# FFN middle tiles copied out of PSUM first, late loads issued after the first U transpose, and one shared tile for the last FFN slice of two chunks

## The chip, the cores and the metric

The kernel runs on one core of a Trainium2 chip. The metric is the device time of one execution in microseconds (us). The kernel before takes 736.66 us as the median of 10 runs (735.02 to 740.17). Five engines work side by side, each through its own list of instructions in order: TensorE (PE in the profile, with its weight loads as PEld), VectorE (DVE), ScalarE (ACT), GpSimd (POOL) and SyncE (SP, which here issues nearly all DMAs). [...]

## The reference

One layer with attention and a feed-forward network (FFN) in parallel on the same normalised input. S = 2048 tokens, D = 640, H = 32 query heads of width 20 that share one key head and one value head, F = 1728.

```
xn  = layernorm(x)                                  # over D, no weights
q   = xn @ wq  -> 32 heads x 20;  k = xn @ wk;  v = xn @ wv
o   = softmax(q k^T / sqrt(20)) v                   # per head, over all 2048 keys
out = x + o @ wo + silu(xn @ w1) @ w2               # w1 640x1728, w2 1728x640
```

The kernel writes silu(h) as 0.5 * h * (1 + tanh(h/2)); the factor 0.5 is applied later, with the residual.

## The kernel before

**Attention, the backbone.** The 2048 queries are cut into 4 chunks of 512 (QW). A unit is one head of one chunk, so there are 128 units, taken three at a time in 43 groups. A group walks over 16 key tiles of 128 (KT), which gives 688 steps. One step (`do_S`) issues three S matmuls (line 773), one per unit, into three PSUM banks, alternating between banks 0 to 2 and 3 to 5. The exponentials of the step are shared out. In a "narrow" step ACT takes two units in one 128x1024 activation (line 791), and DVE takes the third with an integer trick: one `tensor_scalar` out of PSUM (p1, line 805), an offset add on POOL (yp, line 811) and another on DVE for up to three steps at a time (y, `flush_z`, line 873). In a "wide" step ACT takes all three units in one 128x1536 activation and DVE takes none. `want_dve` decides: it adds up how far the planned DVE queue runs behind PE and takes the narrow form if that is below DVE_TH. Then the P·V matmuls (line 861) sum into the U bank (bank 6). At the end of a group DVE copies U to SBUF (`Uev`, line 976), SP issues a DMA transpose of it (`norm_dma`, line 935), POOL gathers the pieces (lines 943 to 948), DVE takes a reciprocal (line 953), and POOL scales (line 962).

**FFN and projections, the filling.** Between the attention steps PE runs jobs (class `Job`), each a chain of matmuls into bank 7, then a `consume` that takes the bank away. Per chunk there are 14 `h_job`s: 5 matmuls of w1 against xnT (line 1090) give a 128x512 tile of h, of which the last, fk = 13, has only 64 rows (FLAST). ACT takes its tanh out of PSUM into the buffer `tb` (line 1098, two slots) and DVE multiplies (line 1103, reading `tb` and PSUM) into `hT`. Bank 7 stays taken until both are done. Then 8 `out_job`s per chunk multiply hT with w2 (line 1152, read out at 1169), and 8 more, a chunk later, multiply the attention output with wo (line 1157, read out at 1187). `qd_job` (lines 1054 and 1061) makes the queries of the coming chunk.

**What sets the order.** `Sched` is a planner that runs when the kernel is built. Every operation has an assumed duration and a priority (a smaller number goes first), and each engine takes the ready operation with the smallest priority. The result is a fixed list per engine. On the chip a late operation holds up all that stands behind it on its engine. PE prefers P·V over jobs when more than NBLK - PV_PRESS of the 31 exponential blocks are in use. On SP, loads named "dma" keep their own order, while the small transposes may overtake them if they are ready and older.

**Late loads.** The FFN's w2 (14 DMAs), wo (5 DMAs) and a 1 MB pre-fill of the second query buffer (`qz(1)`, line 1512) can't start at once, because their SBUF space holds other data in the prologue. `late_loads` is called when the first `qd_job` (c = 0, m = 0) is read out, and waits for that read-out. Five POOL multiplications (line 1522) then scale wo by 2.

```
if c == 0 and m == 0:
    self.late_loads(("qd", sl))
```

Of the kernel before, what the change touches and what calls it, by code (L numbers as in the profile page):

```python
# [14 lines left out]
P = 128  # L15
# [30 lines left out]
NBLK = 31  # L46
NZ = 4
ZB = 3
AHEAD = 30
Q_FROM = 8  # L50
H0_STEP = 10
KT_ACT = ()
Y_POOL = True
Y_TIME = 0.72
Y_LOCK = False
# [5 lines left out]
ZWAIT = 6  # L61
SWITCH = 0.105
S_LEAD = 0.56
PV_PRESS = 8
DVE_TH = 2.6
U_PRIO = 1.1
X_PRIO = 0.8
PACE = (0.9, 0.9, 0.9, 0.9)
# [273 lines left out]


class Job:
    def __init__(self, name, mms, reads, consume, gate=None, min_step=-1, banks=None, on_start=None, width=0, hold=None, use=None):
        self.name = name
        self.mms = mms
        self.reads = reads
        self.consume = consume
        self.gate = gate  # L350
        self.min_step = min_step
        self.on_start = on_start
        self.begun = False
        self.width = width
        self.hold = hold
        self.use = use


class Builder:
# [371 lines left out]
    def do_mm(self, job, now, d):  # L731
        work, fn = job.mms.pop(0)
        job.begun = True
        b = job.bank
        op = self.sc.new("pe", d, lambda pe: fn(pe, b), job.reads, [("B", b)], name=job.name, queue=False)
        op.work = min(work, 0.009) if job.name[0] == "v" else min(work, 0.053) if job.name[0] == "t" else work
        self.pe_mode = "M"
        self.sc.commit(op, now)
        if not job.mms:
            self.cur_job = None  # L740
            job.consume(b)
# [12 lines left out]
    def do_S(self, t, now):  # L754
# [93 lines left out]
        if self.zblocks and (len(self.zblocks) >= (ZB if g < self.NG - 2 else 2) or t - self.zblocks[0][0] >= ZWAIT  # L848
                             or t == self.T - 1 or (kt == KT - 1 and g >= FLUSH_G)):
            self.flush_z()  # L850
        self.move_pv()
        if last:
            self.end_group(g)
# [10 lines left out]
    def flush_z(self):  # L864
# [12 lines left out]
        for i, (t, pv) in enumerate(self.zblocks):  # L877
# [10 lines left out]
                self.pv_mm(pe, 0, 3, kt, x, False, False)  # L888
                return self.pv_mm(pe, 1, 4, kt, x, False, False)
            ts.append((th, ("Y", zs, 1, i), kt))  # L890
        first = self.zblocks[0][1]
        end = self.pv_wait[-1][0].kt == KT - 1
        tail = self.pv_wait.pop() if end else None
        seen = False
# [21 lines left out]
            self.pv_wait.append((op, False))  # L916
        if tail is not None:
            self.pv_wait.append(tail)
        self.zblocks = []

    def can_host(self, op):
        return op.after is not None and not op.after and op.kt < KT
# [8 lines left out]
    def norm_dma(self, g, rows):  # L931
# [5 lines left out]
        op.dur = UT_ISSUE  # L937
        self.ut_cnt[up] += 1
        op.inc_no = self.ut_cnt[up]
        ut = self.UT[:, up, :, :].rearrange("p q (i j) -> p q i j", j=SLOT)  # L940
        w = self.W
        if rows == P:
# [104 lines left out]
    def qd_job(self, c, m, step=-1):  # L1047
        sc = self.sc
        lo, hi = (Q0 if c == 0 else QN)[m]
        rows = hi - lo  # L1050
        mms = []
        for k in range(DC):
            def f(pe, b, k=k):
                return pe.matmul(self.bk(b, 0, QW, 0, rows), self.wq[:, k, lo:hi], self.xnT[:, k, c * QW:(c + 1) * QW],  # L1054
                                 start=(k == 0), stop=(k == DC - 1))
            mms.append((t_mm(QW), f))

        def consume(b):
            sl = self.nqd % 2
            self.nqd += 1  # L1060
            sc.new("dve", t_dve_ps(QW), lambda v: v.tensor_scalar(self.qd[0:rows, sl, :], self.bk(b, 0, QW, 0, rows), C1,
                                                                  None, ALU.mult), [("B", b)], [("qd", sl)],
                   prio=X_PRIO, name=f"qev{c}_{m}")
            sem = sc.sem(f"q{c}_{m}")
            ops = []
            heads = range(lo // DH, -(-hi // DH))
            for h in heads:
                a, z = max(lo, h * DH), min(hi, h * DH + DH)
                r = (h % 4) * SLOT + a - h * DH
                ops.append(sc.dma("sp", lambda q, a=a, z=z, r=r, h=h: q.dma_start(  # L1070
                    self.qT[r:r + z - a, h // 4, c % 2, :], self.qd[a - lo:z - lo, sl, :]), [("qd", sl)],
                    [("qb", c % 2, h)], (z - a) * QW * 2, sem=sem, name="qdma"))
                ops[-1].dur = 0.74
            sc.note(ops[-1], (), [("q", c, h, lo) for h in heads])
            for op in ops:
                op.inc_no = len(ops)
            if c == 0 and m == 0:
                self.late_loads(("qd", sl))
        reads = [("xnT", 4 * c + i) for i in range(4)] + [("wqd", 0), ("wqd", 1)]
        if c >= 2:  # L1080
            step = max(step, self.first_step[c - 1] + KT)
        return Job(f"q{c}_{m}", mms, reads, consume, min_step=step, width=QW if rows == P else 0)

    def h_job(self, c, fk, step):
        sc = self.sc
        rows = P if fk < FC - 1 else FLAST
        mms = []
        for k in range(DC):
            def f(pe, b, k=k):
                return pe.matmul(self.bk(b, 0, QW, 0, rows), self.w1[:, k, fk * P:fk * P + rows],  # L1090
                                 self.xnT[:, k, c * QW:(c + 1) * QW], start=(k == 0), stop=(k == DC - 1))
            mms.append((t_mm(QW), f))

        def consume(b):
            tp = fk % 2
            t = self.tb[0:rows, tp, :]
            src = self.bk(b, 0, QW, 0, rows)
            sc.new("act", t_act(QW), lambda a: a.activation(t, src, AF.Tanh, scale=0.5), [("B", b)], [("tb", tp)],  # L1098
                   prio=X_PRIO, name=f"th{c}_{fk}")
            ks = [("hT", fk)]  # L1100
            if c == 0:
                ks += [("hT_x", i) for i in range(self.XS)]
            sc.new("dve", t_dve_ps(QW), lambda v: v.scalar_tensor_tensor(  # L1103
                out=self.hT[0:rows, fk, :], in0=t, scalar=1.0, in1=src, op0=ALU.add, op1=ALU.mult),
                [("B", b), ("tb", tp)], ks, prio=X_PRIO, name=f"hp{c}_{fk}")
        reads = [("xnT", 4 * c + i) for i in range(4)] + [("w1",)]
        return Job(f"h{c}_{fk}", mms, reads, consume, min_step=step, width=QW if rows == P else 0)

    def try_oT(self, c):
        last = c == QC - 1  # L1110
# [29 lines left out]
    def out_job(self, c, i, e, step=-1, ffn=True, ks=range(DC), src="xres", dst="ost", hmax=H):  # L1140
# [5 lines left out]
        tot = (FC if ffn else 0) + len(ks)  # L1146
        if ffn:
            for fk in range(FC):
                rows = P if fk < FC - 1 else FLAST

                def f(pe, b, fk=fk, rows=rows, m=len(mms)):
                    return pe.matmul(self.bk(b, 0, 320), self.hT[0:rows, fk, i * P:(i + 1) * P],  # L1152
                                     self.w2[0:rows, fk, e0:e0 + 320], start=(m == 0), stop=(m == tot - 1))
                mms.append((t_mm(320), f))
        for k in ks:
            def f(pe, b, k=k, m=len(mms)):
# [76 lines left out]
    def fill_chunk(self, c, t):  # L1233
# [8 lines left out]
        else:  # L1242
            for i in range(4):
                self.load_xres(0, i)
        hs = [(3.0, lambda s, fk=fk: self.h_job(c, fk, s)) for fk in range(FC)]
        if c == 0:
            qs.pop(0)
        ys = []
# [43 lines left out]
    def prologue(self):  # L1292
# [40 lines left out]
        w2p = []  # L1333
        for fk in range(FC):
            rows = P if fk < FC - 1 else FLAST
            w2p.append(lambda q, fk=fk, rows=rows: q.dma_start(self.w2[0:rows, fk, :],
                                                               self.B_w2[fk * P:fk * P + rows, :]))

        def load_w2(extra):
            load_w("sp", "2", w2p, ("w2",), P * D * 2, [("xn", i) for i in range(14)] + [("idf",)], extra)  # L1340
# [322 lines left out]
```

## Time and profile before

| | |
|---|---|
| median of 10 runs | 736.66 us |
| the profiled execution, its own time | 736.84 us |
| its span, first to last instruction | 735.0 us |
| ACT busy | 701.8 us (95%) |
| PE busy | 712.6 us (97%) |
| DVE busy | 650.0 us (88%) |
| POOL busy | 516.0 us (70%) |
| tanh instructions (line 1098) | 56, mean 677 ns |
| FFN products (line 1103) | 56, mean 681 ns |
| narrow exponentials, 128x1024 | 614, mean 1076 ns |
| wide exponentials, 128x1536 | 60, mean 1506 ns |
| exponentials on DVE (line 805) | 626, mean 684 ns |

Busy time is the union of an engine's recorded spans. Spans of neighbouring instructions on ACT and DVE overlap by about a tenth of a microsecond, so the mean of a row is longer than the distance from one start to the next; where it matters, the distance is used. A busy PE isn't PE at its peak: its records are pipelined, and the planner also puts in idle matmuls (lines 697 and 710) to keep PE running. [...]

### The profile page before, as it was taken

The page shows a single profiled execution, that of the slowest core. Times are in us where ns is not written, and L with a number is a line of the kernel's source. Part 1 is how long each engine was busy: PE and PEld are TensorE (multiplying, and loading weights), DVE is VectorE, ACT ScalarE, POOL GpSimd, SP SyncE. Part 2 cuts the span into 40 slices and gives each one's busy share as a digit, 9 for nine tenths or more (in the row PEclk, how much of TensorE's full clock was granted, in tenths as well). Part 3 has the DMA queues.
Part 4 walks back from the last instruction along what each step waited for, and adds up shares of the span by engine and source line. Part 5 has one row for each costly group of instructions (what it writes and reads, how often), then busy time and mean ns, then how long its engine had stood idle before and what let it go on. Part 6 is the DMA issues. An engine that isn't in the chain of part 4 may idle for free.

```text
span 735.0 us, 18718 instructions
## 1 busy us (share of the span) xinstructions
PE 712.6 (97%) x6798; PEld 229.0 (31%) x6798; DVE 650.0 (88%) x1180; ACT 701.8 (95%) x782; POOL 516.0 (70%) x886
## 2 busy tenths in 40 slices
PE   8897999999999999999999999999999999999997
PEld 4431222233332233223332223323333222233334
DVE  7785999989899899999999889999889889899895
ACT  6996999999999999999999999999999999999972
POOL 4366777767787777677778667777687767777763
PEclk9998999999999999999999999999999999999999
DMA  9673000000002011100001111100003001100021
GB/s 272 153 209 93 16 21 16 21 19 16 9 16 45 8 53 39 38 21 1 17 8 30 24 26 53 51 18 8 10 8 45 16 9 47 42 9 8 9 44 37
DMA packets 58465, 29.12 MB, mean 40 GB/s; under 512 B 44390, under 2 KB 57734, under 8 KB 58374
## 3 DMA queue, kind: packets, MB, share of 16 engines
q1 hardware_dynamic: 56918, 27.71, 14.7%
q8 instruction: 55, 0.90, 0.5%
q10 hardware_dynamic: 1456, 0.22, 0.2%
q14 instruction: 36, 0.29, 0.1%
HBM read 11.36 MB, written 2.62 MB: 19 GB/s over the span
## 4 chain that ended last, share of the span: by engine, by line
PE 72%; ACT 16%; DVE 7%; issue 4%; POOL 1%; DVEq 0%; ACTq 0%; POOLq 0%
PE psall L861 24%; PE psall L773 23%; ACT sbt L791 14%; PE psall L1152 10%; PE psall L1090 6%; DVE sbt L805 3%; PE psall L1054 3%; PE psall L1157 2%; ACT sbt L1098 2%; PE psall L710 1%; DVE sbt L873 1%; DVE sbt L976 1%; PE psall L697 1%; ACT sbt L1441 1%; DVE sbt L1421 0%
## 5 line engine op out<-in xcount | busy, mean ns | idle before, releaser
L791 ACT ACTIVATE sbt<-psall 128x1024 bf16<-128x1024 f32 (+2 forms) x688 | 667.2, 1104 | 14.4 <-PE psall L773 12.5
L811 POOL TENSOR_TENSOR sbt<-sbt 128x256 int32<-128x256 int32 x626 | 428.6, 692 | 171.8 <-DVE sbt L805 124.5
L805 DVE TENSOR_SCALAR sbt<-psall 128x512 int16<-128x512 f32 x626 | 418.9, 684 | 46.4 <-PE psall L773 38.6
L773 PE MATMUL psall<-sbt 32*128 32x512 bf16 x2048 | 269.8, 385 | 10.1 <-ACT sbt L791 5.8
L861 PE MATMUL psall<-sbt 128*32 128x512 bf16 x3470 | 263.1, 384 | 4.5 <-POOL sbt L811 4.4
L773 PEld LDWEIGHTS psall<-sbt 32*128 32x128 bf16 x2048 | 69.5, 91 | 252.0 <-ACT sbt L791 86.8
L873 DVE TENSOR_SCALAR sbt<-sbt 128x1536 int16<-128x1536 int16 (+1 forms) x218 | 130.9, 601 | 3.2
L861 PEld LDWEIGHTS psall<-sbt 128*32 128x32 bf16 x3470 | 66.2, 94 | 112.9 <-issue 70.8
L1152 PE MATMUL psall<-sbt 128*128 128x320 bf16 x448 | 87.7, 303 | 0.0
L1090 PE MATMUL psall<-sbt 128*128 128x512 bf16 (+1 forms) x280 | 84.5, 385 | 0.8 <-DVE sbt L1103 0.5
L1152 PEld LDWEIGHTS psall<-sbt 128*128 128x128 bf16 x448 | 33.4, 97 | 44.7 <-issue 35.1
L1103 DVE SCALAR_TENSOR_TENSOR sbt<-sbt,psall 128x512 bf16<-128x512 bf16 (+1 forms) x56 | 38.1, 681 | 8.3 <-ACT sbt L1098 3.8
L1098 ACT ACTIVATE sbt<-psall 128x512 bf16<-128x512 f32 (+1 forms) x56 | 37.9, 677 | 0.0
L1090 PEld LDWEIGHTS psall<-sbt 128*128 128x128 bf16 (+1 forms) x280 | 19.4, 98 | 40.9 <-issue 25.9
L976 DVE CAST sbt<-psall 128x512 bf16<-128x512 f32 x43 | 29.3, 682 | 1.8 <-PE psall L861 1.8
L1157 PE MATMUL psall<-sbt 128*128 128x320 bf16 x144 | 27.8, 302 | 1.4 <-DVE sbt L1135 0.7
L1054 PE MATMUL psall<-sbt 128*128 128x512 bf16 (+1 forms) x95 | 29.1, 385 | 0.0
L962 POOL TENSOR_TENSOR sbt<-sbt 128x240 bf16<-128x240 f32 (+2 forms) x44 | 25.6, 582 | 3.8 <-DVE sbt L953 3.2
L948 POOL TENSOR_TENSOR sbt<-sbt 128x44 f32<-128x44 f32 x84 | 25.2, 300 | 1.1
L946 POOL CAST sbt<-sbt 128x168 f32<-128x168 bf16 x42 | 14.0, 334 | 14.1 <-DMA sbt<-sbt 13.8
L710 PE MATMUL psall<-sbt 128*128 128x512 bf16 (+2 forms) x73 | 18.1, 397 | 2.0 <-POOL sbt L1351 1.5
L1157 PEld LDWEIGHTS psall<-sbt 128*128 128x128 bf16 x144 | 11.4, 97 | 15.5 <-issue 9.8
(86 smaller groups left out, 206.5 us busy)
## 6 DMA issues: line engine op xcount, KB each, us to landing
sbt<-in_A_x_dram SPq DMA_DIRECT2D x32, 160.0 KB, 3.3
out_dram<-sbt SPq DMA_DIRECT2D x15, 160.0 KB, 1.9
sbt<-in_B_w_dram SPq DMA_DIRECT2D x5, 432.0 KB, 6.8
sbt<-sbt SPq DMA_DIRECT2D x105, 20.0 KB
sbt<-in_B_w_dram SPq DMA_DIRECT2D x13, 160.0 KB, 3.0
sbt<-sbt SPq DMA_TRANSPOSE x68, 2.4
sbt<-sbt SPq DMA_DIRECT2D x1, 1024.0 KB, 6.3
sbt<-in_A_wo_dram SPq DMA_DIRECT2D x5, 160.0 KB, 3.0
```

The costliest lines, as they stand in the source:

```text
L773: ins = pe.matmul(self.bk(par3 + j), self.kT[r:r + SLOT, kk, kt * P:(kt + 1) * P], self.qT[r:r + SLOT, h // 4, (x // H) % 2, :], start=Tru ...
L791: return a.activation(self.E[:, b0 * QW:(b0 + na) * QW], self.ps[:, par3 * BANK:(par3 + na) * BANK], AF.Exp, scale=ACT_SCALE)
L805: return v.tensor_scalar(self.Z[:, zs, zp * QW:(zp + 1) * QW], self.bk(bb), 0.0, ZMAX, ALU.max, ALU.min)
L811: sc.new("pool", Y_TIME, lambda v: v.tensor_tensor(self.Y[:, zs, 1, zp * QW:(zp + 1) * QW].bitcast(I32), self.Z[:, zs, zp * QW:(zp + 1) * ...
L861: return pe.matmul(self.bk(UBANK, 0, QW, q * SLOT, (q + 1) * SLOT), self.v[:, w, kt, :], x, start=start, stop=stop, tile_position=(0, q * ...
L873: sc.new("dve", Y_SLOW + t_dve_4x(w), lambda v, k=k: v.tensor_scalar(self.Y[:, zs, k, 0:n * QW], Z, float(PH[k + 1][0]), None, ALU.add), z ...
L1054: return pe.matmul(self.bk(b, 0, QW, 0, rows), self.wq[:, k, lo:hi], self.xnT[:, k, c * QW:(c + 1) * QW], start=(k == 0), stop=(k == DC - 1))
L1090: return pe.matmul(self.bk(b, 0, QW, 0, rows), self.w1[:, k, fk * P:fk * P + rows], self.xnT[:, k, c * QW:(c + 1) * QW], start=(k == 0), s ...
L1098: sc.new("act", t_act(QW), lambda a: a.activation(t, src, AF.Tanh, scale=0.5), [("B", b)], [("tb", tp)], prio=X_PRIO, name=f"th{c}_{fk}")
L1103: sc.new("dve", t_dve_ps(QW), lambda v: v.scalar_tensor_tensor(out=self.hT[0:rows, fk, :], in0=t, scalar=1.0, in1=src, op0=ALU.add, op1=AL ...
L1152: return pe.matmul(self.bk(b, 0, 320), self.hT[0:rows, fk, i * P:(i + 1) * P], self.w2[0:rows, fk, e0:e0 + 320], start=(m == 0), stop=(m = ...
L1157: return pe.matmul(self.bk(b, 0, 320), self.oT[:, k, i * P:(i + 1) * P], self.wo[:, k, e0:e0 + 320], start=(m == 0 and src != "ps"), stop= ...
```

## The change

- **`h_job`.** DVE first copies the h tile from PSUM into `hT` as bf16 (`hc`). Then ACT takes the tanh from that SBUF tile into `tb`, and DVE multiplies `tb` and `hT` in place (`hp`), with the low priority H_PRIO = 3.5. Bank 7 is free after the copy.
- **Paired last tile.** The 64-row tile fk = 13 is computed once for two chunks: two matmuls per k-slice, for chunk c into PSUM rows 0 to 63 and for chunk c + 1 into rows 64 to 127. The odd chunks have 13 h jobs. The last w2 slice is loaded twice, into both halves of the partitions, and `out_job` takes the half that belongs to its chunk.
- **Late loads** are called in `norm_dma` of group 0, behind its U transpose, and wait for that group's U copy.
- **Planner settings.** The first step of each group is always wide (KT_ACT = (0,)), DVE_TH goes from 2.6 to 3.4 us, PV_PRESS from 8 to 12.
- Bookkeeping: `emit_thirds` is split off from `flush_z`, so that left-over P·V pieces are also issued at the end of a group that has no DVE block waiting.

```diff
-KT_ACT = ()
+T_PRIO = 0.8
+H_PRIO = 3.5
+LATE_G = 0
+KT_ACT = (0,)
-PV_PRESS = 8
-DVE_TH = 2.6
+PV_PRESS = 12
+DVE_TH = 3.4
@@ do_S: after the flush_z condition
+        elif last and self.thirds:
+            self.emit_thirds([], None)
@@ norm_dma: after the U transpose is made
+        if g == LATE_G:
+            self.late_loads(("U", up))
@@ qd_job.consume
-            if c == 0 and m == 0:
-                self.late_loads(("qd", sl))
@@ h_job
-        rows = P if fk < FC - 1 else FLAST
+        rows = P
+        pair = fk == FC - 1
...
-                return pe.matmul(self.bk(b, 0, QW, 0, rows), self.w1[:, k, fk * P:fk * P + rows],
-                                 self.xnT[:, k, c * QW:(c + 1) * QW], start=(k == 0), stop=(k == DC - 1))
+                if not pair:
+                    return pe.matmul(self.bk(b), self.w1[:, k, fk * P:(fk + 1) * P], self.xnT[:, k, c * QW:(c + 1) * QW],
+                                     start=(k == 0), stop=(k == DC - 1))
+                for z in range(2):
+                    ins = pe.matmul(self.bk(b, 0, QW, z * FLAST, (z + 1) * FLAST), self.w1[:, k, fk * P:fk * P + FLAST],
+                                    self.xnT[:, k, (c + z) * QW:(c + z + 1) * QW], start=(k == 0), stop=(k == DC - 1),
+                                    tile_position=(0, z * FLAST), skip_group_check=True)
+                return ins
...
-            sc.new("act", t_act(QW), lambda a: a.activation(t, src, AF.Tanh, scale=0.5), [("B", b)], [("tb", tp)],
-                   prio=X_PRIO, name=f"th{c}_{fk}")
...
-            sc.new("dve", t_dve_ps(QW), lambda v: v.scalar_tensor_tensor(
-                out=self.hT[0:rows, fk, :], in0=t, scalar=1.0, in1=src, op0=ALU.add, op1=ALU.mult),
-                [("B", b), ("tb", tp)], ks, prio=X_PRIO, name=f"hp{c}_{fk}")
+            sc.new("dve", t_dve_ps(QW), lambda v: v.tensor_copy(h, self.bk(b)), [("B", b)], ks, prio=X_PRIO,
+                   name=f"hc{c}_{fk}")
+            sc.new("act", t_act(QW), lambda a: a.activation(t, h, AF.Tanh, scale=0.5), [("hT", fk)], [("tb", tp)],
+                   prio=T_PRIO, name=f"th{c}_{fk}")
+            sc.new("dve", t_dve_1x(QW), lambda v: v.scalar_tensor_tensor(
+                out=h, in0=t, scalar=1.0, in1=h, op0=ALU.add, op1=ALU.mult), [("tb", tp), ("hT", fk)], [("hT", fk)],
+                prio=H_PRIO, name=f"hp{c}_{fk}")
@@ out_job
-                rows = P if fk < FC - 1 else FLAST
+                r0 = FLAST * (c % 2) if fk == FC - 1 else 0
+                r1 = r0 + FLAST if fk == FC - 1 else P
@@ fill_chunk
-        hs = [(3.0, lambda s, fk=fk: self.h_job(c, fk, s)) for fk in range(FC)]
+        hs = [(3.0, lambda s, fk=fk: self.h_job(c, fk, s)) for fk in range(FC) if fk < FC - 1 or c % 2 == 0]
@@ prologue, pieces of w2
+            for r0 in ((0,) if rows == P else (0, FLAST)):
+                w2p.append(lambda q, fk=fk, rows=rows, r0=r0: q.dma_start(self.w2[r0:r0 + rows, fk, :],
+                                                                          self.B_w2[fk * P:fk * P + rows, :]))
```

## The prediction

> **What bounds the kernel now.** I read the busy table first, then the groups of instructions with shapes kept apart, then busy time by stretch, then the order of time around the one place that stands out. The busy table names two candidates:
>
> ```profile
> PE 712.6 (97%) x6798; PEld 229.0 (31%) x6798; DVE 650.0 (88%) x1180; ACT 701.8 (95%) x782; POOL 516.0 (70%) x886
> ```
>
> PE's 97% holds pipelined records and idle matmuls, so I test ACT. In order of time its starts are back to back:
>
> ```profile
> 89.60 6.55 ACT L791 ACTIVATE sbt<-psall 128x1024 bf16<-128x1024 f32 x7
> 95.99 0.64 ACT L1098 ACTIVATE sbt<-psall 128x512 bf16<-128x512 f32 x1
> 96.47 3.83 ACT L791 ACTIVATE sbt<-psall 128x1024 bf16<-128x1024 f32 x4
> ```
>
> The tanh starts at 95.99 and the next exponential at 96.47: a tanh costs ACT 0.48 us. Four exponentials and the next tanh's start (100.08) give 3.61/4 = 0.90 us for a narrow one. A wide one is longer by the difference of the means of these two rows, 0.43 us, so 1.33:
>
> ```profile
> L791 ACT ACTIVATE sbt<-psall 128x1024 bf16<-128x1024 f32 x614 | 584.3, 1076 | 12.0 <-PE psall L773 10.5 <-PE psall L861 0.5
> L791 ACT ACTIVATE sbt<-psall 128x1536 bf16<-128x1536 f32 x60 | 89.9, 1506 | 0.0
> L1103 DVE SCALAR_TENSOR_TENSOR sbt<-sbt,psall 128x512 bf16<-128x512 bf16 x52 | 35.4, 681 | 7.9 <-PE psall L773 3.5 <-ACT sbt L1098 3.4
> ```
>
> A group with 15 narrow steps, one wide one and three tanhs needs 15 x 0.90 + 1.33 + 1.43 = 16.3 us of ACT; groups 3, 4 and 6 took 16.5 (from first exponential to first exponential). Groups without a tanh need 14.9 and took 15.0 to 15.7. So ACT sets the pace, and a change is worth what it takes from ACT's own work or from ACT's gaps. Those are 0.1 to 0.8 us in each of the groups 3 to 40, while group 2 took 23.4 us with 16.3 of work. By stretch, that place and the FFN part behind it:
>
> ```profile
> 54.00:70.00 16.00, 11.22 (x89) 2.67 (x84) 8.27 (x15) 10.04 (x11) 9.21 (x17) 0.79 0.41 115
> 81.80:147.50 65.70, 65.48 (x603) 18.56 (x603) 60.95 (x104) 65.70 (x76) 47.71 (x81) 1.00 0.08 20
> ```
>
> The columns are PE, PEld, DVE, ACT and POOL busy, then clock and DMA: ACT is idle for 6.0 us of the first stretch and for nothing in the second. The order of time of SP and then POOL shows why:
>
> ```profile
> 48.58 2.98 SPq L1336 DMA_DIRECT2D sbt<-in_B_w_dram  x6
> 51.61 2.85 SPq L1519 DMA_DIRECT2D sbt<-in_A_wo_dram  x5
> 54.50 0.69 SPq L1512 DMA_DIRECT2D sbt<-sbt  x1
> 55.23 2.30 SPq L935 DMA_TRANSPOSE sbt<-sbt  x1
> ...
> 61.49 0.33 POOL L946 CAST sbt<-sbt 128x168 f32<-128x168 bf16 x1 [6.79 <-DMA sbt<-sbt]
> ```
>
> U of group 0 is copied by 49.89, but its transpose is issued at 55.23, behind the last twelve late loads, and lands 6.2 us later where the median is 2.4, because the 1 MB pre-fill is in front of it. POOL's list has the gather next and stands for 6.79 us; the yp behind it are late, then the P·V that needs them, then S, then ACT:
>
> ```profile
> POOL sbt L946 <- DMA sbt<-sbt: 6.8, 1, 6.8
> PE psall L861 <- POOL sbt L811: 4.4, 1, 4.4
> ACT sbt L791 <- PE psall L773: 6.0, 2, 4.5
> ```
>
> [...] The nearest traced op, the product with a PSUM operand, starts 0.60 before its successor (69.89 to 70.49). The SBUF product isn't in this trace. [...] The old product has one SBUF input and the new one two. [...]
>
> **The change part by part**, against the profiled execution (736.84 us, span 735.0, so 1.8 around the span; the median of the runs is 0.2 below).
>
> *Late loads.* U's transpose is issued at 49.9 and lands at about 52.3 (2.4). Behind it go 15 pieces of w2 at 2.98/6 = 0.50, 5 of wo at 2.85/5 = 0.57, and the pre-fill at 0.69: SP is free at 51.2 + 7.5 + 2.9 + 0.7 = 62.3. What is late next is the second transpose. Its U copy stood at 70.49 in the stalled run, so about 64 without the stall. The pre-fill takes 6.3 us to land by the DMA table, so until 68.5, and the transpose lands about then instead of at 66.4: POOL waits up to 2 us. That doesn't reach ACT: in the old stall POOL stopped at 54.7 and ACT at 60.8, a cushion of 6 us. POOL's five scalings of wo (0.72 each) move to the same place, where POOL is idle for a quarter to a third. w2 is first read at about 150 us, wo and the second query buffer later than 100, so nobody else waits; if the cover were gone each us would be a us. Gain: between 6.0 (ACT's wait) and 6.8 (group 2's gap less a common 0.35), and 3 if part of it comes back at the second transpose. I take **-6.4**.
>
> *Paired tile.* Two of 56 h jobs vanish: 2 x 0.48 = **-1.0** on ACT. Ten PE matmuls go too, hidden under ACT. One 80 KB load is added and counted above.
>
> *Copy first.* ACT: the tanh reads SBUF instead of PSUM. No 512-wide SBUF activation is in the trace[...]. I take 0[...]. DVE: 54 copies at 0.60 (the U copy, line 976, has the same 682 ns) and 54 products at 0.60 replace 56 x 0.60: **+31 us of DVE**. It lies beside ACT if DVE has room. In the FFN stretch above DVE is idle for 4.75 us, and its 104 records overlap by 0.68 - 0.60 = 0.08 or less, so room is 9 at best (counting each op by its distance to the next I get 8.9). Eleven tanhs there add 11 x 0.60 = 6.6 us[...]. DVE is then at 97 to 100% beside an ACT at 100%, tied by two PSUM sets. The tanh also gets a new wait: it stands in ACT's list behind a DVE copy, and all exponentials stand behind it. Gaps: 0 to +5 us; ACT's present gaps in groups 3 to 40 sum to 13.8, and I put a tenth on top: **+1.4**.
>
> *Planner settings.* Of the 60 wide steps 8 are the first eight; the other 52 are one for each of the 42 later groups and ten extra. Forced wide first steps keep 8 + 42 = 50. Against this, planned DVE work in a group with three h jobs and a q job is 15 x 0.60 + 5 x 0.565 + 0.6 + 0.22 + 3 x 1.2 + 0.6 = 16.8 us against 16.3 on ACT; balance needs about half an extra wide step (0.43 on ACT, 0.79 off DVE) per such group, and bursts already made ten. The higher threshold, 0.8, lets about one waiting product (0.6) through. From 50 to 75 wide steps are possible, -4.3 to +6.5 us; I take 65: **+2.1**. PV_PRESS moves PE's order only, under ACT.
>
> Sum: -6.4 - 1.0 + 1.4 + 2.1 = **-3.9**; the profiled execution goes to 732.9 us, the median to **732.7**.
>
> **The rivals.** *DVE fits easily (15%).* Higher threshold and forced steps leave 50 to 54 wide steps (-3 instead of +2) and gaps don't grow: -6.4 - 1.0 - 3 = -10, 726.5. For it: groups without h jobs have 1 to 3.5 us of DVE room. Against it: ten extra wide steps occurred when DVE had more. *DVE eats the gain (15%).* [...]75 wide steps: -6.4 - 1.0 + 6.5 and +1 to +2 for gaps make 0 to +1, so 736.7 to 737.8, no change; with 70 wide steps it ends at 734.5. For it: the 98% above. *ACT waits at every tanh (10%), slower.* If the copy is on average 0.2 us later than planned when ACT comes to the tanh, 54 x 0.2 = +10.8: 743. It decides from (3.9 + 1.5)/54 = 0.10 us a tanh. For it: DVE's list runs up to 3.4 us behind by permission. Against it: the planner places a tanh only after its copy's planned end, and DVE runs to plan (0.60 both). *The stall only moves (part of the second rival):* if the second transpose cost 6 us, 739; the 6 us cushion speaks against it.
>
> **How the numbers follow.** Main case 60%, 730 to 735; others 15, 15, 10. Range 726.5 to 738: leaves out the tanh case and the far ends. A change under 0.2% (1.5 us, 735.2 to 738.1) can't be told from none: faster 0.60 + 0.15 + a third of 0.15 = 0.80, same 0.10, slower 0.10.
>
> **What would show it.** Group 2 near 16.5 us; no POOL wait for a DMA over 3 us; first transpose landing in 2.4 us; 54 tanhs at 0.48 apart; two DVE rows of 54 at about 0.68[...]; 60 to 70 wide steps; ACT's rows naming DVE as releaser for under 2 us. The forecast is wrong if DVE releases ACT for more than 5 us, if wide steps leave 55 to 72, or if POOL waits again at the second transpose.

## The result and the profile after

The changed kernel takes 733.82 us as the median of 14 runs (732.75 to 736.88). The kernel before, run again beside it, takes 737.12 us (51 runs). The ratio is 0.9956, with a 95% interval of 0.9946 to 0.9967: faster by 0.44%, or 3.3 us. The prediction was 732.7, or 3.9 us less than before.

| profiled execution | before | after |
|---|---|---|
| its own time | 736.84 | 734.28 |
| span | 735.0 | 732.5 |
| wide exponentials (128x1536) | 60 | 70 |
| tanhs | 56 | 54 |
| DVE busy | 650.0 | 674.3 |
| first exponential starts at | 16.7 | 17.8 |
| first to last exponential | 704.5 | 702.9 |
| behind the last exponential (the tail) | 13.9 | 11.7 |

The last two rows are the ones to keep in mind: the tail was not in the prediction at all. The start of the first exponential varies from 16.6 to 18.3 us over all kernels of this study, whatever they change, so its 1.2 us here are not read as an effect; they are why the two profiled executions differ by 2.6 us and not by the 3.7 that stretch and tail give.

The busy table, then the groups that answer to those shown of before, in the profile of the changed kernel (L796 is the exponential, L1118 the new copy, L1120 the tanh, L1122 the product):

```profile
PE 712.1 (97%) x6799; PEld 227.3 (31%) x6799; DVE 674.3 (92%) x1220; ACT 707.1 (97%) x780; POOL 526.0 (72%) x875
```

```profile
L796 ACT ACTIVATE sbt<-psall 128x1024 bf16<-128x1024 f32 x605 | 571.2, 1060 | 2.3 <-PE psall L778 1.0 <-PE psall L868 0.5
L796 ACT ACTIVATE sbt<-psall 128x1536 bf16<-128x1536 f32 x70 | 103.0, 1480 | 0.0
L1122 DVE SCALAR_TENSOR_TENSOR sbt<-sbt 128x512 bf16<-128x512 bf16 x54 | 43.5, 805 | 1.2 <-ACT sbt L1120 1.0
L1118 DVE CAST sbt<-psall 128x512 bf16<-128x512 f32 x54 | 36.6, 678 | 0.3 <-PE psall L1102 0.3
L1120 ACT ACTIVATE sbt<-sbt 128x512 bf16<-128x512 bf16 x54 | 35.7, 662 | 2.6 <-DVE sbt L1122 2.2 <-DVE sbt L1118 0.4
```

There are ten wide steps more, not fewer, in spite of the higher threshold. The product takes 805 ns on average where it took 681, and ACT waits for DVE for 2.6 us in all.

The order of time on SP, and POOL's and ACT's waits, show what became of the stall. First SP between 50 and 71 us:

```profile
50.22 1.24 SPq L945 DMA_TRANSPOSE sbt<-sbt  x1
51.80 7.31 SPq L1357 DMA_DIRECT2D sbt<-in_B_w_dram  x15
59.15 2.49 SPq L1540 DMA_DIRECT2D sbt<-in_A_wo_dram  x5
61.68 0.70 SPq L1533 DMA_DIRECT2D sbt<-sbt  x1
62.89 6.51 SPq L1082 DMA_DIRECT2D sbt<-sbt  x7
69.45 1.26 SPq L945 DMA_TRANSPOSE sbt<-sbt  x1
```

```profile
POOL sbt L958 <- DMA sbt<-sbt: 2.2, 1, 2.2
DVE sbt L965 <- POOL sbt L960: 2.1, 1, 2.1
ACT sbt L1120 <- DVE sbt L1122: 2.2, 1, 2.2
```

The first transpose is at once on its way. The second one is late: its U was copied by 66.6, but seven query DMAs, which had queued up behind the late loads, stand in front of it until 69.4. POOL waits 2.2 us for it, DVE's reciprocal stands for 2.1 us on POOL, and ACT, which has a tanh next that needs a `tb` slot, stands for 2.2 us on the DVE product that frees the slot and that is behind the reciprocal. Between the late gather and the reciprocal POOL's list also has three of the five wo scalings, 0.72 us each; no run takes these away alone.

What the copy does to bank 7 stands in the order of time of DVE and ACT in the changed kernel:

```profile
51.35 0.68 DVE L1118 CAST sbt<-psall 128x512 bf16<-128x512 f32 x1
55.14 0.69 DVE L1118 CAST sbt<-psall 128x512 bf16<-128x512 f32 x1
56.75 0.68 ACT L1120 ACTIVATE sbt<-sbt 128x512 bf16<-128x512 bf16 x1
62.73 0.68 DVE L1118 CAST sbt<-psall 128x512 bf16<-128x512 f32 x1
68.65 0.65 ACT L1120 ACTIVATE sbt<-sbt 128x512 bf16<-128x512 bf16 x1
72.79 0.69 ACT L1120 ACTIVATE sbt<-sbt 128x512 bf16<-128x512 bf16 x1
```

By the kernel's own list the three tanhs are those of the h tiles 1, 3 and 0. The tanh of tile 0 comes as late as 72.8, but three tiles have left bank 7 by 63.4. In the kernel before, tile 0 keeps the bank until its tanh and product are done, at 70.6 (shown under late_only). Over all h tiles, bank 7 is held for 1.1 us on average from the end of a tile's last matmul to the end of the last instruction that reads it, against 2.5 us before (worked out from the two traces).

**The ledger.** I go through the exponentials in time order, take each instruction by its distance to the next when nothing waits (narrow 0.904, wide 1.330, tanh 0.477 before and 0.520 after), and call the rest gap. Changes from before to after: wide steps +4.3 and one more narrow step instead of a half one (one unit, 128x512) +0.4; tanhs 54 x 0.520 - 56 x 0.477 = +1.4; gaps in groups 0 to 2 -4.7, in 3 to 40 -0.4, in 41 and 42 -2.5. The sum is -1.5 for the stretch of exponentials. The tail adds -2.2. What made the gaps of groups 41 and 42 smaller was not looked for.

### The profile page after: what moved, and what is told of

It is laid out like the page before. It is cut to its first block, busy times and chain, and to the rows that moved or that the text cites. A ratio compares the mean times of both kernels' runs of the same rounds, so it can differ in the third digit from the quotient of the medians.

```text
span 732.5 us, 18731 instructions
## 1 busy us (share of the span) xinstructions
PE 712.1 (97%) x6799; PEld 227.3 (31%) x6799; DVE 674.3 (92%) x1220; ACT 707.1 (97%) x780; POOL 526.0 (72%) x875
## 4 chain that ended last, share of the span: by engine, by line
PE 41%; ACT 30%; DVE 16%; issue 10%; POOL 2%; DMA 1%; ACTq 0%; DVEq 0%; SPq 0%; POOLq 0%
ACT sbt L796 28%; PE psall L868 14%; PE psall L778 13%; DVE sbt L810 7%; PE psall L1172 4%; PE psall L1102 3%; PE psall L1177 2%; DVE sbt L880 2%; DVE sbt L1122 2%; DVE sbt L1118 2%; PE psall L1066 2%; PE psall L714 2%; ACT sbt L1120 1%; DMA sbt<-sbt 1%; POOL sbt L816 1%
## 5 line engine op out<-in xcount | busy, mean ns | idle before, releaser
L796 ACT ACTIVATE sbt<-psall 128x1024 bf16<-128x1024 f32 (+1 forms) x688 | 667.5, 1094 | 4.9 <-PE psall L778 3.4
L810 DVE TENSOR_SCALAR sbt<-psall 128x512 int16<-128x512 f32 x615 | 408.2, 682 | 31.5 <-PE psall L778 26.2
L880 DVE TENSOR_SCALAR sbt<-sbt 128x1536 int16<-128x1536 int16 (+2 forms) x217 | 132.3, 614 | 2.2
L1102 PE MATMUL psall<-sbt 128*128 128x512 bf16 x260 | 75.8, 384 | 0.9 <-DVE sbt L1118 0.2
L1172 PEld LDWEIGHTS psall<-sbt 128*128 128x128 bf16 x448 | 33.5, 97 | 44.1 <-issue 34.9
L1122 DVE SCALAR_TENSOR_TENSOR sbt<-sbt 128x512 bf16<-128x512 bf16 x54 | 43.5, 805 | 1.2 <-ACT sbt L1120 1.0
L1120 ACT ACTIVATE sbt<-sbt 128x512 bf16<-128x512 bf16 x54 | 35.7, 662 | 2.6 <-DVE sbt L1122 2.2
L1118 DVE CAST sbt<-psall 128x512 bf16<-128x512 f32 x54 | 36.6, 678 | 0.3 <-PE psall L1102 0.3
L988 DVE CAST sbt<-psall 128x512 bf16<-128x512 f32 x43 | 29.3, 681 | 1.4 <-PE psall L868 1.3
L960 POOL TENSOR_TENSOR sbt<-sbt 128x44 f32<-128x44 f32 x84 | 28.8, 343 | 1.0
L1102 PEld LDWEIGHTS psall<-sbt 128*128 128x128 bf16 x260 | 18.2, 97 | 35.3 <-issue 20.4
L1066 PE MATMUL psall<-sbt 128*128 128x512 bf16 (+1 forms) x95 | 27.7, 384 | 0.2 <-DVE sbt L1118 0.2
L714 PE MATMUL psall<-sbt 128*128 128x512 bf16 (+1 forms) x75 | 20.0, 417 | 2.0 <-POOL sbt L1372 1.5
```

The lines of the kernel that those rows point to most:

```text
L796: return a.activation(self.E[:, b0 * QW:(b0 + na) * QW], self.ps[:, par3 * BANK:(par3 + na) * BANK], AF.Exp, scale=ACT_SCALE)
L810: return v.tensor_scalar(self.Z[:, zs, zp * QW:(zp + 1) * QW], self.bk(bb), 0.0, ZMAX, ALU.max, ALU.min)
L880: sc.new("dve", Y_SLOW + t_dve_4x(w), lambda v, k=k: v.tensor_scalar(self.Y[:, zs, k, 0:n * QW], Z, float(PH[k + 1][0]), None, ALU.add), z ...
L1102: return pe.matmul(self.bk(b), self.w1[:, k, fk * P:(fk + 1) * P], self.xnT[:, k, c * QW:(c + 1) * QW], start=(k == 0), stop=(k == DC - 1))
L1118: sc.new("dve", t_dve_ps(QW), lambda v: v.tensor_copy(h, self.bk(b)), [("B", b)], ks, prio=X_PRIO, name=f"hc{c}_{fk}")
L1120: sc.new("act", t_act(QW), lambda a: a.activation(t, h, AF.Tanh, scale=0.5), [("hT", fk)], [("tb", tp)], prio=T_PRIO, name=f"th{c}_{fk}")
```

## The experiments

Twelve more kernels were run beside the kernel before. In this table "stretch" is first to last exponential, "tail" what lies behind it, both of the profiled execution. "F left" counts the 320-wide matmuls that the kernel's own list has behind the last S matmul, those with w2 and those with wo together; the recorded texts call them all the FFN's second half. Of the 34 before, 10 are w2's; of the 8 in the changed kernel none is, so its FFN is finished by then.

| kernel | median us | ratio to before, 95% | wide | stretch | F left | tail |
|---|---|---|---|---|---|---|
| before | 737.12 | 1 | 60 | 704.5 | 34 | 13.9 |
| changed | 733.82 | 0.9956 (0.9946 to 0.9967) | 70 | 702.9 | 8 | 11.7 |
| late_only | 742.94 | 1.0072 (1.0053 to 1.0091) | 60 | 702.8 | 90 | 21.6 |
| settings_only | 741.24 | 1.0042 (1.0024 to 1.0060) | 49 | 697.6 | 101 | 23.8 |
| copy_only | 748.62 | 1.0160 (1.0137 to 1.0183) | 96 | 720.9 | 9 | 11.1 |
| undo_copy | 735.97 | 0.9981 (0.9970 to 0.9991) | 49 | 689.7 | 113 | 25.7 |
| undo_late | 741.52 | 1.0053 (1.0033 to 1.0073) | 66 | 710.0 | 21 | 12.7 |
| product_psum | 758.32 | 1.0291 (1.0273 to 1.0309) | 58 | 698.4 | 151 | 41.7 |
| copy_two_chunks | 732.94 | 0.9941 (0.9926 to 0.9955) | 60 | 698.4 | 31 | 13.6 |
| unpair | 737.35 | 0.9997 (0.9987 to 1.0008) | 69 | 706.2 | 21 | 12.8 |
| press_8 | 736.52 | 0.9991 (0.9980 to 1.0003) | 71 | 706.3 | 10 | 10.3 |
| split_late | 733.38 | 0.9952 (0.9936 to 0.9969) | 71 | 702.5 | 8 | 9.9 |
| split_late_2 | 730.84 | 0.9912 (0.9893 to 0.9932) | 68 | 699.5 | 8 | 11.5 |
| half_copy | 727.98 | 0.9872 (0.9852 to 0.9893) | 54 | 696.3 | 18 | 12.1 |

### One part alone, on the kernel before

**late_only.** The late loads behind group 0's U transpose, nothing else.

```diff
+LATE_G = 0
...
@@ qd_job.consume
-            if c == 0 and m == 0:
-                self.late_loads(("qd", sl))
@@ norm_dma
+        if g == LATE_G:
+            self.late_loads(("U", up))
```

> The kernel before with the late loads moved behind the U transpose of group 0, and nothing else. Its list has 60 wide steps, as before. Theory A (the move is the main gain, and a part of it comes back at the second transpose, because SP then issues the query DMAs late): ACT's idle time between 54 and 82 us falls from 6 to about 2 us, and the time falls by 4 to 5 us. Theory B (as the prediction had it, the second transpose is covered): 6 to 6.8 us. Theory C (the gain comes from the FFN part and the settings): under 1.5 us.

All three were wrong: the time rose by 0.72%. ACT's gaps in groups 0 to 2 did fall, from 9.1 to 5.0 us, which is what theory A names. But the tail grew from 13.9 to 21.6 us. PE's order of time behind the last S shows what fills it (L1153 is the FFN's second half; in the kernel before, ten such matmuls stand there, up to 723.8):

```profile
719.60 2.24 PE L862 MATMUL psall<-sbt 128*32 128x512 bf16 x28
721.77 1.12 PE L1153 MATMUL psall<-sbt 128*128 128x320 bf16 x7
722.73 0.28 PE L991 MATMUL psall<-sbt 128*128 128x64 bf16 x4
722.85 2.79 PE L1153 MATMUL psall<-sbt 128*128 128x320 bf16 x17
725.57 0.40 PE L1131 MATMUL psall<-sbt 128*128 128x128 bf16 x4
725.80 6.39 PE L1153 MATMUL psall<-sbt 128*128 128x320 bf16 x42
```

So the jobs had not kept up with the attention. The first job was late already. These lines are of the kernel before, PE and ACT in order of time:

```profile
44.38 1.04 PE L1090 MATMUL psall<-sbt 128*128 128x512 bf16 x4
68.70 0.59 ACT L1098 ACTIVATE sbt<-psall 128x512 bf16<-128x512 f32 x1
70.63 0.39 PE L1090 MATMUL psall<-sbt 128*128 128x512 bf16 x1 [0.52 <-DVE sbt L1103]
```

The first h tile is in bank 7 by 46 us, but its tanh runs at 68.7, and until then no other job can have the bank. The code tells why: this tanh writes `tb` slot 0, which the 1 MB pre-fill reads, so the planner puts it behind the landing that it assumes for the pre-fill (60.4 in its own time before, 70.1 in late_only). On the chip the pre-fill lands at 60.8 before and at 69.7 in late_only, and the tanh runs at 68.7 and 75.6: what it waits for there is its place in ACT's list, and ACT is behind the plan. Moving the pre-fill moves the tanh: in split_late_2 below it is issued at 51.1 instead of 61.7, and tile 0's tanh runs at 58.7 instead of 72.8. The jobs behind don't catch up. The first tanh of late_only is 7 us later than before, the 14th 17 us and the last 32 us (689 instead of 657); why the delay grows isn't shown.

**settings_only.** The planner settings, nothing else (with `emit_thirds`).

```diff
-KT_ACT = ()
+KT_ACT = (0,)
...
-PV_PRESS = 8
-DVE_TH = 2.6
+PV_PRESS = 12
+DVE_TH = 3.4
...
```

> The kernel before with KT_ACT = (0,), DVE_TH 3.4, PV_PRESS 12 (and the left-over P.V pieces issued at a group's end), and nothing else. Its list has 49 wide steps against 60. Theory A (the settings are worth what they take from ACT): 11 x 0.43 = 4.7 us, the time falls by 3.5 to 5 us. Rival (DVE can't keep up with 637 blocks and ACT's gaps grow by as much): within 1.5 us of before, with ACT's waits on PE over 15 us.

Both were wrong. The stretch fell by 6.9 us, more than the eleven wide steps' 4.7, and the tail grew by 9.9 us: 0.42% slower. The three settings were not taken apart on this kernel.

**copy_only.** The new `h_job` read-out alone.

```diff
...
+            sc.new("dve", t_dve_ps(QW), lambda v: v.tensor_copy(h, src), [("B", b)], ks, prio=X_PRIO,
...
+            sc.new("act", t_act(QW), lambda a: a.activation(t, h, AF.Tanh, scale=0.5), [("hT", fk)], [("tb", tp)],
...
+            sc.new("dve", t_dve_1x(QW), lambda v: v.scalar_tensor_tensor(
+                out=h, in0=t, scalar=1.0, in1=h, op0=ALU.add, op1=ALU.mult), [("tb", tp), ("hT", fk)], [("hT", fk)],
...
```

> The kernel before with h_job's copy first, tanh and product from SBUF (with the new priorities), and nothing else; DVE_TH stays 2.6. Its list has 96 wide steps against 60 and 590 DVE blocks against 626. Theory A (the added DVE work is paid by ACT in wide steps): 36 x 0.43 = 15 us on ACT, the time rises by 10 to 16 us. Rival (bank 7 free early shortens the waits of PE enough to make up for it): within 2 us of before.

Theory A holds: 1.6% slower, and the stretch is longer by 16.4 us for 36 wide steps. Its tail, though, is the shortest of these three, 11.1 us.

Each of the three parts by itself makes the kernel slower, by 5.7, 4.0 and 11.4 us against their common runs of before (737.24). Together, with the pair, they make it faster by 3.3.

### One part undone, on the changed kernel

**undo_copy.** Tanh and product out of PSUM again; late loads, pair and settings stay.

```diff
-            sc.new("dve", t_dve_ps(QW), lambda v: v.tensor_copy(h, self.bk(b)), [("B", b)], ks, prio=X_PRIO,
-                   name=f"hc{c}_{fk}")
-            sc.new("act", t_act(QW), lambda a: a.activation(t, h, AF.Tanh, scale=0.5), [("hT", fk)], [("tb", tp)],
+            sc.new("act", t_act(QW), lambda a: a.activation(t, src, AF.Tanh, scale=0.5), [("B", b)], [("tb", tp)],
...
-                out=h, in0=t, scalar=1.0, in1=h, op0=ALU.add, op1=ALU.mult), [("tb", tp), ("hT", fk)], [("hT", fk)],
+                out=self.hT[:, fk, :], in0=t, scalar=1.0, in1=src, op0=ALU.add, op1=ALU.mult),
```

> The changed kernel with tanh and product out of PSUM again; the paired tile, the late loads and the settings stay. Its list has 49 wide steps against 70. Theory A (the copy costs more than it gives): 21 x 0.43 = 9 us less on ACT, the time is 724 to 728 us. Rival (the copy is what lets the other parts work, since bank 7 held through tanh and product stalls PE): 732 us or more.

735.97 lies in the rival's range, but theory A's saving is there too. The stretch is 13.3 us shorter than in the changed kernel; theory A had 9 of that. The tail is 14.0 us longer. ACT's waits show it as one wait of 21.2 us, that of the first output read-out for PE, where the changed kernel has 7.0 (the second line):

```profile
ACT sbt L1203 <- PE psall L1176: 21.2, 1, 21.2
ACT sbt L1204 <- PE psall L1177: 7.0, 1, 7.0
```

and PE's order of time in that wait is FFN work, then the output work that the changed kernel had begun before the last S:

```profile
709.71 1.33 PE L1171 MATMUL psall<-sbt 128*128 128x320 bf16 x7
710.88 0.28 PE L1000 MATMUL psall<-sbt 128*128 128x64 bf16 x4
710.99 1.49 PE L1171 MATMUL psall<-sbt 128*128 128x320 bf16 x9
712.41 0.40 PE L1148 MATMUL psall<-sbt 128*128 128x128 bf16 x4
712.65 10.61 PE L1171 MATMUL psall<-sbt 128*128 128x320 bf16 x70
723.19 2.35 PE L1176 MATMUL psall<-sbt 128*128 128x320 bf16 x16
```

This gave **theory D**: the time is ACT's own work, plus ACT's gaps at the first U transposes, plus a tail of about 11.7 us and 0.13 us for each of these matmuls left over (10.61 us for 70 is 0.15; from 8 left to 113 the tail grows by 14.0, so 0.13).

**undo_late.** The late loads back at the first query read-out, the rest as changed.

```diff
-        if g == LATE_G:
-            self.late_loads(("U", up))
...
+            if c == 0 and m == 0:
+                self.late_loads(("qd", sl))
```

> The changed kernel with the late loads back at the read-out of the first query job; everything else stays. Its list has 66 wide steps (changed kernel 70) and 21 matmuls of the FFN's second half behind the last S (8). Theory D (three terms: ACT's own work, ACT's gap at the first U transposes, and a tail of about 11.7 us plus 0.13 us for each of those matmuls over 8): -4 x 0.43 + 4.4 for the gap + 1.7 for the tail, so 4 to 5 us above the changed kernel, 737 to 739. Theory C (the move is worth nothing): 732 to 734.

7.7 us above the changed kernel, more than theory D's 4 to 5, and theory C is out. The stall is back, and longer; ACT's gaps in groups 0 to 2 are 10.4 us:

```profile
POOL sbt L956 <- DMA sbt<-sbt: 19.0, 16, 8.1
DVE sbt L963 <- POOL sbt L958: 8.9, 8, 6.7
```

So the same move costs 5.7 us in the kernel before, where bank 7 is held through tanh and product, and gives 7.7 us in the changed one, where the copy frees it. The two kernels differ in the pair and the settings too; undo_copy, which has these and the move but not the copy, has its first tanh at 75 us and the long tail. The gaps of the groups behind grew by 3.4 us too; why isn't known.

**product_psum.** The product reads h from PSUM, so bank 7 is held to the end. Each h tile still has its copy, tanh and product.

```diff
-                out=h, in0=t, scalar=1.0, in1=h, op0=ALU.add, op1=ALU.mult), [("tb", tp), ("hT", fk)], [("hT", fk)],
+                out=h, in0=t, scalar=1.0, in1=self.bk(b), op0=ALU.add, op1=ALU.mult), [("B", b), ("tb", tp), ("hT", fk)], [("hT", fk)],
```

> The changed kernel, but the product reads h from PSUM instead of SBUF, so bank 7 stays taken until the product is done, as before the change (the copy and the tanh from SBUF stay). Same instructions, same number of DVE operations. Its list has 58 wide steps, and 151 second-half matmuls and 25 of the first half behind the last S. Theory D (the copy's worth is that it frees bank 7): the time after the last exponential grows from 11.7 to over 30 us, the whole to 745 us or more. Rival (the bank is no limit and DVE's load decides): 58 instead of 70 wide steps give 5 us, so 728 to 730. [...]the product row falls from a mean of 805 ns to about 685 if the second SBUF input is what costs 0.12 us, and stays near 800 if not.

Theory D, clearly: the tail is 41.7 us although the stretch is 4.5 us shorter. The 41.7 is more than the copy is worth: the product keeps its low priority H_PRIO here, and bank 7 is held for 3.7 us on average, longer than in the kernel before and in undo_copy (2.5 each). It also gives the price of the second SBUF input by itself, with the two product rows alike but for that input:

```profile
L1122 DVE SCALAR_TENSOR_TENSOR sbt<-sbt,psall 128x512 bf16<-128x512 bf16 x54 | 36.6, 679 | 3.6 <-ACT sbt L1120 2.9
```

679 ns against 805: the second SBUF input costs 0.126 us on average, with POOL busy 72% of the time in the changed kernel (68% here). In the changed kernel's trace the long products are those with POOL's work beside them: of its 54 the four with no POOL instruction beside them took 679 to 693 ns, the 44 with 0.3 us or more of POOL's work beside them 825 on average, from 623 to 1126. With the second input in PSUM, all 54 took 679 on average.

**unpair.** The 64-row tile for each chunk by itself.

```diff
-        pair = fk == FC - 1
+        pair = False
...
-        hs = [(3.0, lambda s, fk=fk: self.h_job(c, fk, s)) for fk in range(FC) if fk < FC - 1 or c % 2 == 0]
+        hs = [(3.0, lambda s, fk=fk: self.h_job(c, fk, s)) for fk in range(FC)]
```

> The changed kernel with the 64-row tile computed for each chunk by itself, as before the change (56 h jobs, 14 w2 loads); all else stays. Its list has 69 wide steps (changed kernel 70), 56 tanhs, and 21 second-half matmuls behind the last S (8). Theory D: +2 x 0.48 for the tanhs, +1.7 for the tail, -0.4 for the wide step, so 2 to 2.5 us above the changed kernel, 736 us. Rival (the pair is worth its two tanhs alone): 1 us, 734.8.

3.5 us above the changed kernel, more than theory D's 2 to 2.5 and far from the rival's 1, so all of the change's gain goes with it. The tail grew by 1.1 and the two tanhs cost 1.0. ACT's gaps grew by 3.1 in all, for which no cause is known; one wide step fewer, and a half step more in place of a narrow one, give 0.8 back.

**press_8.** PV_PRESS back at 8.

```diff
-PV_PRESS = 12
+PV_PRESS = 8
```

> The changed kernel with PV_PRESS back at 8, so that PE takes jobs for longer before it prefers P.V; all else stays. Its list has 71 wide steps and 10 second-half matmuls behind the last S, nearly as the changed kernel. Theory E (as in the prediction, the setting moves only PE's order, under ACT): 734 to 735. Rival (P.V that comes late holds exponential blocks, and ACT's gaps grow): 736 us or more, with ACT's gaps in groups 3 to 40 over 17 us (changed kernel 14.9).

2.7 us above the changed kernel, with gaps of 17.0 us in groups 3 to 40 (14.9, both with a tanh taken as 0.477). Theory E is out, and the rival's numbers came: the setting that makes PE prefer P·V isn't free of ACT. ACT's waits for S rose to 6.0 us from the 3.4 of the changed kernel:

```profile
ACT sbt L796 <- PE psall L778: 6.0, 13, 1.4
```

That exponential blocks held by late P·V are behind these waits, as the rival has it, isn't shown.

### Sizes and moves

**copy_two_chunks.** The copy in chunks 0 and 1 only; from chunk 2 on, tanh and product read PSUM as in the kernel before.

```diff
+            if c < 2:
+                sc.new("dve", t_dve_ps(QW), lambda v: v.tensor_copy(h, self.bk(b)), [("B", b)], ks, prio=X_PRIO,
...
+            else:
+                src = self.bk(b)
+                sc.new("act", t_act(QW), lambda a: a.activation(t, src, AF.Tanh, scale=0.5), [("B", b)], [("tb", tp)],
...
```

> The changed kernel with the copy only in chunks 0 and 1; chunks 2 and 3 take tanh and product out of PSUM as before. Its list has 60 wide steps and 31 second-half matmuls behind the last S. Theory D: -10 x 0.43 for the wide steps, +3.0 for the tail, so 1 to 2 us under the changed kernel, 731.5 to 733. Rival (only the last chunk's copy shortens the tail, so the tail is as long as without any copy, 25 us): 740 or more.

732.94, inside theory D's range. The jobs are one chain: time saved in the first two chunks still shortens the tail at the end.

**split_late** and **split_late_2.** The late loads spread over three groups: behind the transposes of groups 0, 1 and 2 go w2, wo and the pre-fill in split_late, and the pre-fill, wo and w2 in split_late_2.

> The changed kernel with the late loads in three parts: w2 behind the U transpose of group 0, wo behind that of group 1, the 1 MB pre-fill behind that of group 2. Its list has 71 wide steps and 8 second-half matmuls behind the last S. Theory A (SP's queue of late loads pushes the query DMAs into the second U transpose, and POOL's 2.2 us wait there reaches ACT through DVE's reciprocal): POOL's wait at the second transpose falls under 0.5 us, ACT's gap in group 2 from 2.7 to about 0.5, the time by 1.5 to 2.5 us, to 731.5 to 732.5. Rival (the 2.7 us gap has another cause, such as the five tanhs of that group): unchanged, 733.5 to 734.5.

ACT's gap in group 2 fell from 2.7 to 0.3 us, as theory A has it, and the profiled execution took 732.35 us (734.28 for the changed kernel). But the median, 733.38, misses theory A's range and can't be told from the changed kernel's. Of the 2.3 us that groups 0 to 2 gave, the stretch keeps only 0.5: gaps in later groups and one wide step more took the rest, and why isn't known. In this kernel the pre-fill comes behind the first tanhs, which overwrite `tb` slot 0, so it spreads a tanh tile in place of its constant, and the kernel doesn't compute the reference; only its times are read here. (The text on record for split_late_2 says that the pre-fill overwrote queries; the list shows otherwise, since the query DMAs of chunk 1 come later.)

In split_late_2 the order is turned round (split_late has (0, 1, 2)); `late_loads` is cut into three parts:

```diff
-LATE_G = 0
+LATE_GS = (2, 1, 0)
...
-        if g == LATE_G:
-            self.late_loads(("U", up))
+        if g in LATE_GS:
+            self.late_loads(("U", up), LATE_GS.index(g))
...
```

> The changed kernel with the 1 MB pre-fill behind the U transpose of group 0, wo behind that of group 1 and w2 behind that of group 2. (In the run split_late the pre-fill came after the first query DMAs of chunk 1 and overwrote them, so its output lacked those queries; here the order is the changed kernel's.) 68 wide steps, 8 second-half matmuls behind the last S. Theory A: ACT's gap in group 2 falls from 2.7 to about 0.5 us, two wide steps fewer give 0.9, so 730.5 to 732. Rival: the gap only moves to the group that now has the w2 loads: 733 to 734.

730.84, inside theory A's range: the gap in group 2 is 0.4 us, and it didn't move on to group 3 (1.1 against 1.0). The wo scalings also come a group later in both split kernels, so the late transpose and these scalings aren't told apart.

**half_copy.** On top of split_late_2, only every second h tile is copied first, and PV_PRESS is 10.

```diff
-PV_PRESS = 12
+PV_PRESS = 10
...
+            if (c + fk) % 2 == 0:
+                sc.new("dve", t_dve_ps(QW), lambda v: v.tensor_copy(h, self.bk(b)), [("B", b)], ks, prio=X_PRIO,
...
+            else:
+                src = self.bk(b)
+                sc.new("act", t_act(QW), lambda a: a.activation(t, src, AF.Tanh, scale=0.5), [("B", b)], [("tb", tp)],
...
```

> As split_late_2, but only every second h tile (c + fk even) is copied first, the others take tanh and product out of PSUM as before the change, and PV_PRESS is 10. Its list has 54 wide steps (changed kernel 70) and 18 second-half matmuls behind the last S. Theory D: -16 x 0.43 for the wide steps, +1.3 for the tail, -2.2 for the gap in group 2, so 725.5 to 728 us, faster than both kernels. Rival (half the tiles holding bank 7 makes ACT's gaps grow by what the wide steps give): 731 us or more.

727.98 us, in theory D's range, ratio 0.9872 to before: it beats both kernels, and is 0.8% below the changed one. Its two product rows and its exponentials:

```profile
L796 ACT ACTIVATE sbt<-psall 128x1536 bf16<-128x1536 f32 x54 | 79.2, 1474 | 1.2 <-PE psall L778 1.1
L1123 DVE SCALAR_TENSOR_TENSOR sbt<-sbt 128x512 bf16<-128x512 bf16 x26 | 21.8, 837 | 1.3 <-ACT sbt L1121 0.9
L1133 DVE SCALAR_TENSOR_TENSOR sbt<-sbt,psall 128x512 bf16<-128x512 bf16 x28 | 19.0, 678 | 0.9 <-ACT sbt L1128 0.3 <-PE psall L778 0.2
```

It has 54 wide steps, nearly as few as without any copy, and a tail of 12.1 us, nearly as short as with all. Against split_late_2 two things differ, the copy and PV_PRESS; their shares of the 2.9 us were not taken apart.

## Why the prediction was right, and where it wasn't

The time and the sign were right, and the size was off by 0.6 us. That agreement is luck. Measured in the ledger, the terms that the prediction had sum to about +0.9 us: late loads -4.7, the pair's tanhs -1.0, the copy +2.3 for the tanhs and -0.4 for the gaps, the settings +4.7 for wide steps and the half step. What puts the changed kernel ahead is the tail, -2.2, and the gaps of groups 41 and 42, -2.5; the prediction had neither.

- **What bounds the kernel.** ACT does set the pace of the stretch: in each of the fourteen kernels its gaps are under 5% of it. The step that failed is that a change is worth only what it takes from ACT's work or gaps. There is a second chain, the jobs through bank 7. In the kernel before it has no slack, and what is left of it when the last exponential is done is in the tail. The prediction held the tail fixed. It names neither what frees bank 7, nor how late the first tanh is (68.7), nor PE's waits for the product, which stood in the trace of before:

```profile
PEld psall L1090 <- DVE sbt L1103: 6.7, 14, 0.8
```

- **Late loads, -6.4.** The size was off: -4.7 in the gaps of groups 0 to 2, inside the bounds of 3 and 6.8. POOL did wait again at the second transpose, which the prediction had named as a sign of being wrong. The transpose was late by about 2 us, but for another reason than the pre-fill: the seven query DMAs on SP. (In late_only, undo_copy and product_psum, where it is issued right behind the pre-fill, it does land late, after 5.7 to 5.8 us.) The sentence that a 2 us wait doesn't reach ACT was wrong. The cushion of 6 us was read from POOL's stop and ACT's stop; in this case DVE's own list was held by its reciprocal, and the 2.2 us went straight through. split_late_2 takes that part too.
- **Paired tile, -1.0.** unpair puts it at 3.5. Both traces have 280 matmuls for the h tiles, so none goes; but the two of a pair start 3 to 4 ns apart in the trace, and the ten pairs keep PE busy for 2.7 us, where the twenty single ones of before took 6.2. What goes besides the tanhs is two passes through bank 7, a saving that the prediction put at nothing.
- **Copy first: ACT.** The tanh from SBUF was taken at no cost. That was the author's estimate; the trace of before has no such tanh. It costs 0.043 us more: 0.520 against 0.477 from start to start, 2.3 us for 54.
- **Copy first: DVE.** +31 us of work was right: busy time rose by 24.3, with eleven exponentials (7.5) handed to ACT. The second SBUF input costs 0.126 us a product (805 ns against 679 in product_psum). The upper end of the predicted 97 to 100% for DVE was the author's estimate; nothing in the trace of before shows a product with two SBUF inputs. Gaps did not grow (+1.4 predicted, -0.4 in groups 3 to 40). The copy itself was booked as pure cost. undo_copy shows the other side: in the changed kernel it costs ACT 13.3 us of stretch and takes 14.0 us off the tail.
- **Settings, +2.1.** 70 wide steps instead of 65: +4.3. That PV_PRESS moves PE's order only, under ACT, was wrong by 2.7 us.
- **Rivals.** DVE fits easily: no, 70 wide steps. DVE eats the gain: with 70 wide steps it was to end at 734.5, close to what was measured, but by growing gaps, which didn't come. ACT waits at every tanh: no, ACT's waits for DVE at the tanhs are 2.6 us in all, of which 2.2 are the one wait at the second transpose. None of them was the tail; that three of the parts are each slower alone was nowhere in the prediction.

What stays open: the 3.1 us of gaps in unpair, the 3.4 us in undo_late, the 2.5 us of groups 41 and 42, and why a late first tanh grows into a later last one.

## What to carry to other kernels

An engine that is nearly always busy, as ACT is here at 95 and 97%, tells only the time of the stretch that it covers: look at what runs behind its last instruction, and ask which work there was meant to be finished earlier and which buffer held it up. Here the wide steps and the matmuls left behind the last S can both be counted in the list before a run; the later expectations used these counts, the prediction didn't. Freeing a buffer early has a price, and in this case it paid only where the chain through the buffer would else have fallen behind: copy_only shortened the tail by 2.8 us and lost 16.4 in the stretch. A little of it can go a long way: with every second tile copied (and PV_PRESS at 10) the tail stayed nearly as short with half of the copies. Parts of a change that shift work between two tight chains can each lose alone and win together, so undo one part from the whole as well as trying each by itself.

## What the runs showed of the hardware

- An ACT tanh of 128x512 costs 0.043 us more out of SBUF (bf16, changed kernel) than out of PSUM (f32, before): back to back, 0.520 against 0.477 in the median from its start to the next one's.
- A DVE product of 128x512 bf16 with both inputs in SBUF runs for 805 ns on average in the changed kernel, and for 679 with one of them in PSUM (product_psum), with GpSimd busy for 72 and 68% of the time. half_copy has both kinds in one kernel: 837 and 678, with GpSimd at 73%. The four with no GpSimd instruction beside them in the changed kernel took 679 to 693 ns, and the next instruction started 0.60 to 0.61 us after their start; with one input in PSUM (before) it is 0.60 in the median.
- The U transpose landed in 2.4 us in the median, and in 6.2 us in the kernel before where SP issued it, at 55.2, right behind the 1 MB SBUF to SBUF pre-fill (issued at 54.5, landed at 60.8). Seven query DMAs of 20 KB or less took SP 5.4 us (from 40.3) and 6.5 us (from 62.9) to issue in the changed kernel, 0.77 to 0.93 us each; the transpose behind the second seven, its U copied by 66.6, was issued at 69.4.
- Two 64-row matmuls of one k-slice, one into PSUM rows 0 to 63 and one into 64 to 127, start 3 to 4 ns apart. Where no other matmul comes between, the next pair follows 0.21 to 0.24 us later, as the next single one does in the kernel before. The ten pairs of the changed kernel keep PE busy for 2.7 us, where the twenty single ones of the kernel before took 6.2.
